# Decode layer on one core: paired copies of transposed K, constants on GpSimd, aligned programs, and w_gate's first row in two pieces

## The chip, the cores and the metric

The kernel runs on one core of one Trainium2 chip. The metric is device time in microseconds of one execution. A comparison of kernels uses the median of several executions on the same chip.

## The reference

One token for each of two batch entries goes through an attention layer and a feed-forward layer. All inputs are bf16; D = 640, 32 heads of 192, a cache of 8192 positions of which the last 2048 are used, F = 1536.

```python
def _A_ref(x, k_cache, v_cache, wq, wo):      # B=2, Sq=1, D=640, Hq=Hkv=32, Sk=8192, Dh=192
    W = min(4096, max(256, Sk // 4))          # 2048
    q = (x @ wq).reshape(B, Sq, 32, 192).transpose(0, 2, 1, 3)
    k = k_cache[:, :, Sk - W:, :]
    v = v_cache[:, :, Sk - W:, :]
    p = _softmax(einsum("bhqd,bhkd->bhqk", q, k) * (192 ** -0.5))
    o = einsum("bhqk,bhkd->bhqd", p, v)
    return o.transpose(0, 2, 1, 3).reshape(B, Sq, 32 * 192) @ wo

def _B_ref(x, w_gate, w_up, w_down):
    return (_gelu(x @ w_gate) * (x @ w_up)) @ w_down

h = x + _A_ref(_layernorm(x), k_cache, v_cache, wq, wo)
out = h + _B_ref(_layernorm(h), w_gate, w_up, w_down)
```

Nearly all of the work is reading: 16 loads of K and 16 of V of 3 MB each, wq (7.5 MB), wo (four loads of 1.9 MB), and the three feed-forward matrices of 1.9 MB each.

## The kernel before

**Groups.** The 2 x 32 heads are worked in 16 groups (NG) of four heads of one batch entry. J counts blocks of four groups. For group g, one load brings K of the four heads into a ring in SBUF (128 partitions, 24576 bytes each), another brings V.

**Per group.** `transposes(g, half)` turns K on TensorE, two bf16 at a time as one f32, 48 transposes of 128x128 per group: twelve steps n, each of four transposes into one of four PSUM banks `tps[0..3]` in turn, and then one copy of 128x1024 bf16 into `ktr`, by ScalarE (ACT) for n in (2, 3, 5, 8, 11) and by VectorE (DVE) for the other seven. `scores(g)` multiplies `ktr` by the masked query `rq` (made four groups ahead by `q_masked` on GpSimd). DVE takes the maximum, `softmax(g)` takes the exponent on ACT, `e_columns(g)` turns it, and `pv(g)` multiplies by V. The order on TensorE is: first half of the transposes of g, `e_columns(g-1)`, second half, `pv(g-1)`, `scores(g)`, `softmax(g)`. After every fourth group `z_rows`, `o_rows`, `o_columns` and `oproj` normalise the block and add its part of `@ wo`.

**Who orders what.** `_Prog` records the operations of each engine in program order and works out which semaphore waits are needed; `emit` writes the program of one engine, and `emit_loop` writes that of TensorE as a loop over J with four passes. `load` puts a transfer on a list, and `pump` issues it on SyncE's queue (SP) as soon as the ring bytes that it overwrites have been used, in the order of the list: K0, wq, K1, V0, K2, V1 and so on, then wo, w_gate, w_up and w_down. ACT issues two transfers of its own at the very start: `load_wg0` (L379), row 0 of each partition's five rows of w_gate into its own tile `wgh`, 128 partitions of 3072 bytes, and x into `xrow`.

**Constants.** Masks, selectors and identity matrices are made on the chip. GpSimd makes index ramps (`ci`, `pi`, `ei`), bit masks (`bits`) and zeros; DVE makes everything else from them between the first layer norm and the first K copies, and a second set in `consts_late`, recorded after `q_stationary` and ahead of `scores(0)`.

**The end.** After group 15: `e_columns(15)`, `z_rows(3)`, `pv(15)`, `o_rows(3)`, `oproj(2)`, `o_columns(3)`, `oproj(3)`, the second layer norm, the gate product (`ffn_in`, which reads `wgh` first), the up product, and w_down in four pieces, each as soon as it has landed. DVE copies the result (L862) and SP sends it out (L863).

Of the kernel before, what the change touches and what calls it, by code (L numbers as in the profile page):

```python
# [216 lines left out]
TPG = 64  # L217
WDC = ((0, 6), (6, 9), (9, 11), (11, 12))
# [9 lines left out]
def bass_sequential_preLN__sliding_block_cached__geglu_ffn__decode_kernel(  # L228
# [12 lines left out]
    with ExitStack() as ctx:  # L241
# [79 lines left out]
        tps = [ps(f"tps{i}", [128, 512], F32) for i in range(4)]  # L321
# [123 lines left out]
        dve(lambda e: e.memset(eps_t[:, :], EPS), W=["eps"])  # L445
        dve(lambda e: e.memset(onesd[:, :], 1.0 / D), W=["onesd"])
        act(lambda e: e.preload_act_table_set("natural_log_exp_and_others"))


        dve(lambda e: e.memset(xnT[:, :, :].rearrange("p a b -> p (a b)").bitcast(I32), 0), W=["xnT"])  # L450
# [21 lines left out]
        def _x_T(e):  # L472
# [10 lines left out]
        dve(tt(pti[:, :], pi[:, :].to_broadcast([128, 11]), bits[:, :], ALU.bitwise_and),  # L483
            R=["pi"] + [("bits", k) for k in range(11)], W=["pti"])
        dve(lambda e: e.tensor_copy(pf[:, :], pti[:, :]), R=["pti"], W=["pf"])
# [10 lines left out]
        dve(ts(pg[:, 1:2], rb(31), 16.0, ALU.is_lt), R=["pf"], W=["v16"])  # L496
        dve(ts(pg[:, 2:3], rb(31), 4.0, ALU.is_lt), R=["pf"], W=["v4"])
        dve(ts(pg[:, 4:5], rb(16), 8.0, ALU.mult, rb(3), ALU.add), R=["pf"], W=["c16"])
        dve(ts(pg[:, 5:6], rb(96), 0.125, ALU.mult, pg[:, 4:5], ALU.add), R=["pf", "c16"], W=["c16b"])
        dve(ts(pg[:, 6:7], rb(96), 0.5, ALU.mult, rb(1), ALU.add), R=["pf"], W=["c64"])  # L500
        dve(ts(pg[:, 7:8], rb(12), 0.5, ALU.mult, pg[:, 6:7], ALU.add), R=["pf", "c64"], W=["c64b"])
        dve(ts(pg[:, 6:7], rb(2), 4.0, ALU.mult, pg[:, 7:8], ALU.add), R=["pf", "c64b"], W=["c64"])
        dve(ts(pg[:, 7:8], rb(16), 64.0, ALU.mult, pg[:, 6:7], ALU.add), R=["pf", "c64"], W=["c64b"])
        dve(ts(pg[:, 8:9], rb(96), 1.0 / 32.0, ALU.mult), R=["pf"], W=["cq"])
        dve(ts(pg[:, 9:10], rb(6), rb(1), ALU.add), R=["pf"], W=["cqa"])
        dve(ts(pg[:, 9:10], pg[:, 9:10], 4.0, ALU.mult, pg[:, 8:9], ALU.add), R=["cqa", "cq"], W=["cqb"])
        dve(ts(pg[:, 10:11], rb(64), 1.0 / 16.0, ALU.mult, rb(31), ALU.add), R=["pf"], W=["chd"])
        dve(ts(pg[:, 11:12], rb(3), 2.0, ALU.mult), R=["pf"], W=["p3"])
        dve(ts(pg[:, 12:13], rb(32), rb(31), ALU.add, 16.0, ALU.mult), R=["pf"], W=["c63"])

        dve(ts(selq[:, :], cf[:, 0, 0:32], pg[:, 9:10], ALU.is_equal), R=["cf0", "cqb"], W=["selq"])
        dve(lambda e: e.tensor_copy(ef[:, :], ei[:, :]), R=["ei"], W=["ef"])
        for r in range(5):
            dve(ts(ge[:, :, r], ef[:, :], 192.0 * r, ALU.is_ge), R=["ef"], W=[("ge", r)])
        dve(tt(mask[:, :, :], ge[:, :, 0:4], ge[:, :, 1:5], ALU.subtract), R=[("ge", r) for r in range(5)], W=["mask"])

        dve(ts(pm[:, :], cf[:, 3, :], rb(28), ALU.is_equal), R=["cfm", "pf"], W=["pm"])
        dve(ts(oh16[:, :], cf[:, 0, 0:16], pg[:, 5:6], ALU.is_equal), R=["cf0", "c16b"], W=["oh16"])
        dve(ts(sel64[:, :], cf[:, 0, 0:64], pg[:, 7:8], ALU.is_equal), R=["cf0", "c64b"], W=["sel64"])
        dve(ts(mask16[:, :], cf[:, 2, 0:16], pg[:, 11:12], ALU.is_equal), R=["cfm", "p3"], W=["mask16"])  # L520
        dve(ts(mska[:, :], cf[:, 1, :], 4.0, ALU.mult, rb(12), ALU.is_equal), R=["cfm", "pf"], W=["mska"])
        dve(ts(zsel[:, :], mska[:, :], pg[:, 1:2], ALU.mult), R=["mska", "v16"], W=["zsel"])
        dve(ts(mska[:, :], mska[:, :], -1.0, ALU.add, BIG, ALU.mult), R=["mska", "zsel"], W=["mska"])

        dve(lambda e: e.memset(lsx[:, :, :], 0.0), W=["lsx"])
        dve(lambda e: e.memset(sps[:, :], 0.0), X=["s"])
        dve(lambda e: e.memset(m1[:, :], 0.0), X=["m1"])

        def consts_late():
            dve(ts(oh4[:, :], cf[:, 0, 0:4], pg[:, 8:9], ALU.is_equal), R=["cf0", "cq"], W=["oh4"])  # L530
            dve(ts(cf[:, 1, :], cf[:, 1, :], 2.0, ALU.mult), R=["cfm", "mska"], W=["cf1"])
            dve(ts(cf[:, 4, :], cf[:, 4, :], 0.25, ALU.mult), R=["cfm"], W=["cf4"])
            dve(tt(cf[:, 1, :], cf[:, 1, :], cf[:, 4, :], ALU.add), R=["cf1", "cf4"], W=["cf1"])
            dve(ts(cf[:, 3, :], cf[:, 3, :], 1000.0, ALU.mult), R=["cfm", "pm"], W=["cf3"])
            dve(tt(cf[:, 1, :], cf[:, 1, :], cf[:, 3, :], ALU.add), R=["cf1", "cf3"], W=["cf1"])
            for tp in range(2):
                dve(ts(selw[:, tp, :], cf[:, 1, :], float(tp), ALU.add, rb(31), ALU.is_equal), R=["cf1", "pf"], W=[("selw", tp)])
            dve(ts(bsel[:, :], cf[:, 0, 0:2], rb(31), ALU.is_equal, 1.0 / D, ALU.mult), R=["cf0", "pf"], W=["bsel"])
            for h in range(2):
                dve(ts(hsel[:, h, :], cf[:, 0, 0:17], 512.0 * h, ALU.add, pg[:, 12:13], ALU.is_equal), R=["cf0", "c63"], W=[("hsel", h)])  # L540
            dve(ts(pg[:, 8:9], rb(32), 1.0 / 32.0, ALU.mult), R=["pf", "cqb", "oh4"], W=["cb"])
            dve(ts(selb[:, :], cf[:, 0, 0:2], pg[:, 8:9], ALU.is_equal, pg[:, 2:3], ALU.mult), R=["cf0", "cb", "v4"], W=["selb"])
            dve(ts(maskhd[:, :], cf[:, 0, 0:8], pg[:, 10:11], ALU.is_equal, pg[:, 2:3], ALU.mult),
                R=["cf0", "chd", "v4"], W=["maskhd"])
# [4 lines left out]
        def transposes(g, half):  # L549

            kk, ktoks = where["k", g]
            kv = kk.bitcast(F32)
            for n in range(6 * half, 6 * half + 6):
                c, ch = n % 3, n // 3
                bi = tb_count[0] % 4
                tb_count[0] += 1

                def fn(e, c=c, ch=ch, bi=bi):
                    for u in range(4):
                        off = 128 * (3 * (4 * ch + u) + c)  # L560
                        ins = e.transpose(tps[bi][:, 128 * u:128 * (u + 1)], kv[:, off:off + 128], identf[:, :])  # L561
                    return ins

                pe(fn, R=ktoks + ["identf"], X=[("t", bi)])
                if n == 11:
                    done(("k", g))
                bv = tps[bi][:, :].bitcast(BF16)
                dst = ktr[:, c, 1024 * ch:1024 * (ch + 1)]
                if n in (2, 3, 5, 8, 11):
                    act(lambda e, dst=dst, bv=bv: e.activation(out=dst, in_=bv, func=ACT.Copy),  # L570
                        W=[("kt", n)], X=[("t", bi)])
                else:
                    dve(lambda e, dst=dst, bv=bv: e.tensor_copy(dst, bv), W=[("kt", n)], X=[("t", bi)], cls=0)  # L573
# [41 lines left out]
        def scores(g):  # L615
# [8 lines left out]
            pe(fn, R=[("rq", g % 4)] + [("kt", n) for n in range(12)], X=["s"])  # L624
# [242 lines left out]
        P.resolve({("dve", 0): 4 * 11, ("dve", 1): 8, ("act", 0): 4 * 6, ("pool", 0): 4})  # L867
# [40 lines left out]
```

## Time and profile before

| | |
|---|---|
| median of 3 runs (lowest to highest) | 292.94 us (292.78 to 292.95) |
| the profiled execution | 293.0 us, of which its span is 291.4 |
| mean granted TensorE clock | 0.858 |
| moved by DMA | 122.44 MB, 420 GB/s over the span |
| busy: PE, DVE, ACT, POOL | 194.3, 128.6, 96.0, 8.6 us |
| K transposes on PE (L561) | 768 in 114.9 us; idle before them 45.7, of it 42.9 for K's loads |
| K copies on DVE (L573) and ACT (L570) | 112 of 688 ns, 80 of 1023 ns |

The profile is of one execution. "Busy" is the sum of an engine's instructions. A line of the page's groups gives line, engine, operation, the tiles out<-in, how many, the busy time, the mean of one, and then the idle time of the engine just before them with what ended most of it. In the DMA section, q1 is SP's queue, q10 ACT's, and "instruction" marks transfers that bring program code. The chain is followed back from the last instruction, at each step to what released it.

### The profile page before, as it was taken

What the parts mean: (1) busy time and instruction counts of PE and PEld (TensorE: products, weight loads), DVE (VectorE), ACT (ScalarE), POOL (GpSimd) and SP (SyncE); (2) the same over time, 40 slices, a digit from 0 to 9 for tenths busy, and PEclk for the clock granted to TensorE, in tenths of its full rate; (3) what the DMA queues carried; (4) which work ended last, traced back from release to release, by engine and by line L of the source; (5) the groups of instructions that cost most, each with busy time, mean ns of one, the idle gap of its engine ahead of it and who ended that gap; (6) DMA issues with size and microseconds to landing.
All of it is one profiled execution on the core that took longest, in us unless ns stands there. A gap on an engine that the chain in (4) does not pass through costs nothing.

```text
span 291.4 us, 5056 instructions
## 1 busy us (share of the span) xinstructions
PE 194.3 (67%) x2141; PEld 150.9 (52%) x2141; DVE 128.6 (44%) x311; ACT 96.0 (33%) x120; POOL 8.6 (3%) x36
## 2 busy tenths in 40 slices
PE   1570759747768197849496496749496977494585
PEld 1560436727466195628284475447475855472342
DVE  4761075623537144616156154434365534352332
ACT  1142016623442143616143063416161634251001
POOL 4000020000000000000000000000000000000000
PEclk9998699995979579998869599968897799897955
DMA  8999999999999999999999999999999999999994
GB/s 324 432 440 422 427 432 431 428 427 432 427 418 441 432 432 430 428 432 432 432 413 449 428 428 428 432 432 428 428 432 425 432 432 432 432 428 419 421 414 174
DMA packets 6506, 122.44 MB, mean 420 GB/s; under 512 B 734, under 2 KB 864, under 8 KB 1504
## 3 DMA queue, kind: packets, MB, share of 16 engines
q1 hardware_dynamic: 6348, 121.90, 97.8%
q10 hardware_dynamic: 148, 0.40, 0.5%
q8 instruction: 7, 0.11, 0.2%
q14 instruction: 3, 0.02, 0.0%
HBM read 122.29 MB, written 0.00 MB: 420 GB/s over the span
## 4 chain that ended last, share of the span: by engine, by line
DMA 76%; PE 19%; SPq 2%; DVE 1%; issue 0%
DMA ring<-in_A_k_cache_dram 57%; PE tps L561 15%; DMA ring<-in_A_wq_dram 10%; DMA ring<-in_B_w_down_dram 9%; PE tps L582 2%; SPq L348 2%; PE ops L663 1%; PE m L714 1%; PE m L696 1%; DVE ktr L573 0%; DVE ering L413 0%; PE m L856 0%; PE m L647 0%; PE m L677 0%; DVE yrow L862 0%
## 5 line engine op out<-in xcount | busy, mean ns | idle before, releaser
L561 PE MATMUL tps<-identf,ring 128*128 128x128 f32 x768 | 114.9, 318 | 45.7 <-DMA ring<-in_A_k_cache_dram 42.9
L561 PEld LDWEIGHTS tps<-identf,ring 128*128 128x128 f32 x768 | 106.1, 167 | 49.3 <-DMA ring<-in_A_k_cache_dram 44.2
L570 ACT ACTIVATE ktr<-tps 128x1024 bf16<-128x1024 bf16 x80 | 79.2, 1023 | 85.0 <-PE tps L561 85.0
L573 DVE COPY ktr<-tps 128x1024 bf16<-128x1024 bf16 x112 | 74.4, 688 | 72.9 <-PE tps L561 72.2
L638 ACT ACTIVATE eexp<-sm,nm 128x512 bf16<-128x512 f32 x16 | 11.5, 721 | 65.2 <-DVE nm L636 65.2
L663 PE MATMUL ops<-ring,ering 128*32 128x384 bf16 x512 | 25.0, 340 | 6.0 <-DMA ring<-in_A_v_cache_dram 6.0
L627 DVE CUSTOM_DVE_ANT_1 sm<-sps,mska 128x512 f32<-128x512 f32 x16 | 11.1, 691 | 35.9 <-PE sps L619 35.9
L619 PE MATMUL sps<-ktr,rq 128*16 128x512 bf16 x384 | 24.6, 388 | 1.1 <-POOL rq L413 1.1
L663 PEld LDWEIGHTS ops<-ring,ering 128*32 128x32 bf16 x512 | 12.7, 99 | 14.8 <-DMA ring<-in_A_v_cache_dram 7.6
L619 PEld LDWEIGHTS sps<-ktr,rq 128*16 128x16 bf16 x384 | 9.2, 88 | 11.4 <-POOL rq L413 1.2
L634 PEld LDWEIGHTS m<-mrhs,pm 128*128 128x128 bf16 x16 | 1.5, 95 | 23.4 <-DVE mrhs L409 23.4
L634 PE MATMUL m<-mrhs,pm 128*128 128x16 bf16 x16 | 2.9, 183 | 15.7 <-DVE mrhs L409 15.7
L413 POOL TENSOR_TENSOR rq<-qs,mask 128x96 bf16<-128x96 bf16 x16 | 5.6, 359 | 195.5 <-PE sps L619 161.3
L582 PE MATMUL tps<-ring,xnT 128*32 128x384 bf16 x80 | 5.5, 455 | 7.7 <-DMA ring<-in_A_wq_dram 7.7
L582 PEld LDWEIGHTS tps<-ring,xnT 128*32 128x32 bf16 x80 | 3.1, 131 | 9.9 <-issue 7.9
L413 DVE TENSOR_TENSOR ering<-m,mask 128x256 bf16<-128x256 f32 x16 | 6.7, 419 | 2.2 <-PE m L647 2.0
L605 DVE CAST qs<-ops 128x384 bf16<-128x384 f32 x1 | 0.6, 558 | 14.1 <-PE ops L600 14.1
L714 PE MATMUL m<-ring,ot 128*2 128x320 bf16 x96 | 4.1, 307 | 2.5 <-DMA ring<-in_A_wo_dram 2.5
L794 ACT ACTIVATE lnv<-tps,eps_t 98x1 f32<-98x1 f32 x1 | 0.3, 261 | 16.6 <-PE tps L792 16.6
L647 PE MATMUL m<-sel,eexp 128*128 128x64 bf16 x64 | 4.7, 200 | 1.2 <-ACT eexp L638 1.2
L413 DVE TENSOR_TENSOR orow<-m,wm 128x1536 bf16<-128x1536 f32 x3 | 5.3, 1751 | 0.0
L673 DVE COPY osb<-ops 128x192 f32<-128x192 f32 x8 | 2.5, 353 | 6.0 <-PE ops L663 6.0
(126 smaller groups left out, 85.6 us busy)
## 6 DMA issues: line engine op xcount, KB each, us to landing
ring<-in_A_k_cache_dram SPq DMA_DIRECT2D x16, 3072.0 KB, 31.7
ring<-in_A_v_cache_dram SPq DMA_DIRECT2D x16, 3072.0 KB, 27.4
ring<-in_A_wq_dram SPq DMA_DIRECT2D x1, 7680.0 KB, 28.6
ring<-in_A_wo_dram SPq DMA_DIRECT2D x4, 1920.0 KB, 21.9
ring<-in_B_w_gate_dram SPq DMA_DIRECT2D x1, 1536.0 KB, 31.5
ring<-in_B_w_up_dram SPq DMA_DIRECT2D x1, 1536.0 KB, 23.8
ring<-in_B_w_down_dram SPq DMA_DIRECT2D x1, 960.0 KB, 26.3
ring<-in_B_w_down_dram SPq DMA_DIRECT2D x1, 480.0 KB, 27.0
```

Source lines behind the costliest of these rows:

```text
L348: P.op("sp", lambda e, v=v, src=src: e.dma_start(v, src), W=toks + [("sem", sem)], dma=sem)
L413: return lambda e: e.tensor_tensor(out=out, in0=a, in1=b, op=op)
L561: ins = e.transpose(tps[bi][:, 128 * u:128 * (u + 1)], kv[:, off:off + 128], identf[:, :])
L570: act(lambda e, dst=dst, bv=bv: e.activation(out=dst, in_=bv, func=ACT.Copy), W=[("kt", n)], X=[("t", bi)])
L573: dve(lambda e, dst=dst, bv=bv: e.tensor_copy(dst, bv), W=[("kt", n)], X=[("t", bi)], cls=0)
L582: ins = e.matmul(tps[0][32 * r:32 * (r + 1), 0:384], lhsT=xnT[:, c, 32 * J:32 * (J + 1)], rhs=wq[:, c, 1536 * J + 384 * r:1536 * J + 384 * ...
L619: ins = e.matmul(sps[32 * ch:32 * ch + 16, :], lhsT=rq[:, g % 4, k, :], rhs=ktr[:, k // 2, 1024 * ch + k % 2:1024 * (ch + 1):2], start=(k ...
L627: dve(lambda e: e.tensor_tensor_reduce(out=sm[:, :].rearrange("p (u x) -> p u x", u=4), in0=sps[:, :].rearrange("p (u x) -> p u x", u=4), ...
L638: act(lambda e: e.activation(out=eexp[:, :], in_=sm[:, :], func=ACT.Exp, bias=nm[:, 0:1], scale=1.0, accum_out=zr[:, g % 4:g % 4 + 1]), R= ...
L647: ins = e.matmul(o, lhsT=eexp[:, 128 * u:128 * (u + 1)], rhs=sel64[:, :], start=True, stop=True)
L663: ins = e.matmul(ops_[32 * r:32 * (r + 1), 0:384], lhsT=ering[:, g % 4, t, :], rhs=vv[:, 384 * t:384 * (t + 1)], start=(g % 4 == 0 and t < 4),
L714: ins = e.matmul(m1[32 * r:32 * r + 2, 192:512], lhsT=ot[:, kk, :], rhs=wo[:, kk - k0, 320 * h:320 * (h + 1)], start=(kk == 1 or J < 2 and ...
```

## The change

Four things change.

- The four PSUM banks become two tiles `tpp[0..1]` of two banks each. `transposes` now has three steps per half, each of eight transposes into one of the two tiles, and one copy of 128x2048: DVE for the first and third step (channels 0 and 1 of one quarter), ACT for the middle one (channel 2 of two quarters).
- The constants that DVE made, all but the first few, are made by GpSimd; four of them directly as index ramps instead of by masking bits. Some memsets and the bit tests on DVE move ahead of the identity matrix.
- `addr_align` places what follows it in the programs of GpSimd, DVE and ACT at a fixed place against a block of 128 instructions: GpSimd and ACT at its start, DVE at place 120. For ACT it stands behind its DMA issues. At most two fillers are executed; a longer gap is jumped over.
- `load_wg0` issues two transfers, partitions 100 to 127 and then 0 to 99, with a semaphore each, instead of one of 128.

```diff
+WGP = 100
...
-        tps = [ps(f"tps{i}", [128, 512], F32) for i in range(4)]
+        tpp = [ps(f"tpp{i}", [128, 1024], F32) for i in range(2)]
+        tps = [tpp[i // 2][:, 512 * (i % 2):512 * (i % 2 + 1)] for i in range(4)]
...
         def load_wg0():
-            where["wg", 0] = wgh[:, :, :], ["wgh"]
-            P.op("act", lambda e: e.dma_start(wgh[:, 0, :], B_w_gate.rearrange("(p c) f -> p c f", c=NC5)[:, 0, :]), W=["wgh"], dma="wg0")
+            where["wg", 0] = wgh[:, :, :], [("wgh", 0), ("wgh", 1)]
+            src = B_w_gate.rearrange("(p c) f -> p c f", c=NC5)
+            for i, (p0, p1) in enumerate(((WGP, 128), (0, WGP))):
+                P.op("act", lambda e, p0=p0, p1=p1: e.dma_start(wgh[p0:p1, 0, :], src[p0:p1, 0, :]), W=[("wgh", i)], dma=f"wg0{i}")
...
+        dve(lambda e: e.memset(eps_t[:, :], EPS), W=["eps"])
+        dve(lambda e: e.memset(onesd[:, :], 1.0 / D), W=["onesd"])
+        dve(lambda e: e.memset(xnT[:, :, :].rearrange("p a b -> p (a b)").bitcast(I32), 0), W=["xnT"])
+        dve(lambda e: e.memset(lsx[:, :, :], 0.0), W=["lsx"])
+        dve(lambda e: e.memset(sps[:, :], 0.0), X=["s"])
+        dve(lambda e: e.memset(m1[:, :], 0.0), X=["m1"])
         dve(lambda e: e.tensor_copy(cf[:, 0, :], ci[:, :]), R=["ci"], W=["cf0"])
         dve(lambda e: e.tensor_copy(pg[:, 0:1], pi[:, :]), R=["pi"], W=["row"])
+        dve(tt(pti[:, :], pi[:, :].to_broadcast([128, 11]), bits[:, :], ALU.bitwise_and),
+            R=["pi"] + [("bits", k) for k in range(11)], W=["pti"])
+        dve(lambda e: e.tensor_copy(pf[:, :], pti[:, :]), R=["pti"], W=["pf"])
...
-        for k, m in enumerate((3, 6, 28, 96)):
-            dve(ts(cti[:, k, :], ci[:, :], m, ALU.bitwise_and), R=["ci"], W=[("cti", k)])
-        dve(lambda e: e.tensor_copy(cf[:, 1:5, :], cti[:, :, :]), R=[("cti", k) for k in range(4)], W=["cfm"])
+        for k, pat in enumerate(([[0, 32], [1, 4]], [[0, 16], [2, 4], [0, 2]], [[0, 4], [4, 8], [0, 4]], [[32, 4], [0, 32]])):
+            pool(lambda e, k=k, pat=pat: e.iota(cti[:, k, :], pattern=pat, base=0, channel_multiplier=0), W=[("cti", k)])
+        pool(lambda e: e.tensor_copy(cf[:, 1:5, :], cti[:, :, :]), R=[("cti", k) for k in range(4)], W=["cfm"])
...
-        dve(ts(selq[:, :], cf[:, 0, 0:32], pg[:, 9:10], ALU.is_equal), R=["cf0", "cqb"], W=["selq"])
+        pool(ts(selq[:, :], cf[:, 0, 0:32], pg[:, 9:10], ALU.is_equal), R=["cf0", "cqb"], W=["selq"])
...
         def consts_late():
-            dve(ts(oh4[:, :], cf[:, 0, 0:4], pg[:, 8:9], ALU.is_equal), R=["cf0", "cq"], W=["oh4"])
+            pool(ts(oh4[:, :], cf[:, 0, 0:4], pg[:, 8:9], ALU.is_equal), R=["cf0", "cq"], W=["oh4"])
...
-            for n in range(6 * half, 6 * half + 6):
-                c, ch = n % 3, n // 3
-                bi = tb_count[0] % 4
+            for k in range(3):
+                bi = tb_count[0] % 2
                 tb_count[0] += 1
+                banks = [(2, 2 * half), (2, 2 * half + 1)] if k == 1 else [(0, 2 * half + k // 2), (1, 2 * half + k // 2)]
...
-                if n in (2, 3, 5, 8, 11):
-                    act(lambda e, dst=dst, bv=bv: e.activation(out=dst, in_=bv, func=ACT.Copy),
-                        W=[("kt", n)], X=[("t", bi)])
+                bv = tpp[bi][:, :].bitcast(BF16)
+                if k == 1:
+                    dst = ktr[:, 2, 2048 * half:2048 * (half + 1)]
+                    act(lambda e, dst=dst, bv=bv: e.activation(out=dst, in_=bv, func=ACT.Copy), W=[("kt", half, k)], X=both)
                 else:
-                    dve(lambda e, dst=dst, bv=bv: e.tensor_copy(dst, bv), W=[("kt", n)], X=[("t", bi)], cls=0)
+                    ch = 2 * half + k // 2
+                    dst = ktr[:, 0:2, 1024 * ch:1024 * (ch + 1)]
+                    dve(lambda e, dst=dst, bv=bv: e.tensor_copy(dst, bv.rearrange("p (a x) -> p a x", a=2)), W=[("kt", half, k)],
+                        X=both, cls=0)
...
+        nc.gpsimd.addr_align(128, 0, 2)
         P.emit("pool", nc.gpsimd, sems)
+        nc.vector.addr_align(128, 120, 2)
         P.emit("dve", nc.vector, sems)
-        P.emit("act", nc.scalar, sems)
+        P.emit("act", nc.scalar, sems, P.per["act"][:3])
+        nc.scalar.addr_align(128, 0, 2)
+        P.emit("act", nc.scalar, sems, P.per["act"][3:])
```

The lines left out move the other constants from `dve(...)` to `pool(...)` unchanged.

More of the change, by code (lines that the diff above doesn't have):

```diff
@@ L512, in bass_sequential_preLN__sliding_block_cached__geglu_ffn__decode_kernel @@
-        dve(lambda e: e.tensor_copy(ef[:, :], ei[:, :]), R=["ei"], W=["ef"])
-        for r in range(5):
[L514 to L518, printed above, removed]
@@ new lines, in bass_sequential_preLN__sliding_block_cached__geglu_ffn__decode_kernel @@
+        pool(ts(pg[:, 7:8], rb(12), 0.5, ALU.mult, pg[:, 6:7], ALU.add), R=["pf", "c64"], W=["c64b"])
+        pool(ts(pg[:, 6:7], rb(2), 4.0, ALU.mult, pg[:, 7:8], ALU.add), R=["pf", "c64b"], W=["c64"])
+        pool(ts(pg[:, 7:8], rb(16), 64.0, ALU.mult, pg[:, 6:7], ALU.add), R=["pf", "c64"], W=["c64b"])
+        pool(ts(pg[:, 8:9], rb(96), 1.0 / 32.0, ALU.mult), R=["pf"], W=["cq"])
+        pool(ts(pg[:, 9:10], rb(6), rb(1), ALU.add), R=["pf"], W=["cqa"])
+        pool(ts(pg[:, 9:10], pg[:, 9:10], 4.0, ALU.mult, pg[:, 8:9], ALU.add), R=["cqa", "cq"], W=["cqb"])
@@ new lines, in bass_sequential_preLN__sliding_block_cached__geglu_ffn__decode_kernel @@
+        pool(tt(mask[:, :, :], ge[:, :, 0:4], ge[:, :, 1:5], ALU.subtract), R=[("ge", r) for r in range(5)], W=["mask"])
+        pool(ts(pm[:, :], cf[:, 3, :], rb(28), ALU.is_equal), R=["cfm", "pf"], W=["pm"])
+        pool(ts(oh16[:, :], cf[:, 0, 0:16], pg[:, 5:6], ALU.is_equal), R=["cf0", "c16b"], W=["oh16"])
+        pool(ts(sel64[:, :], cf[:, 0, 0:64], pg[:, 7:8], ALU.is_equal), R=["cf0", "c64b"], W=["sel64"])
+        pool(ts(mask16[:, :], cf[:, 2, 0:16], pg[:, 11:12], ALU.is_equal), R=["cfm", "p3"], W=["mask16"])
@@ L544, in consts_late @@
+            pool(ts(pg[:, 8:9], rb(32), 1.0 / 32.0, ALU.mult), R=["pf", "cqb", "oh4"], W=["cb"])
+            pool(ts(selb[:, :], cf[:, 0, 0:2], pg[:, 8:9], ALU.is_equal, pg[:, 2:3], ALU.mult), R=["cf0", "cb", "v4"], W=["selb"])
+            pool(ts(maskhd[:, :], cf[:, 0, 0:8], pg[:, 10:11], ALU.is_equal, pg[:, 2:3], ALU.mult),
                 R=["cf0", "chd", "v4"], W=["maskhd"])
@@ L552, in transposes, with fn @@
             kv = kk.bitcast(F32)
-            for n in range(6 * half, 6 * half + 6):
-                c, ch = n % 3, n // 3
-                bi = tb_count[0] % 4
+            for k in range(3):
+                bi = tb_count[0] % 2
                 tb_count[0] += 1
[L558 to L561, printed above, removed]
-                    return ins
-                pe(fn, R=ktoks + ["identf"], X=[("t", bi)])
-                if n == 11:
+                banks = [(2, 2 * half), (2, 2 * half + 1)] if k == 1 else [(0, 2 * half + k // 2), (1, 2 * half + k // 2)]
+                def fn(e, banks=banks, bi=bi):
+                    for j, (c, ch) in enumerate(banks):
+                        for u in range(4):
+                            off = 128 * (3 * (4 * ch + u) + c)
+                            ins = e.transpose(tpp[bi][:, 512 * j + 128 * u:512 * j + 128 * (u + 1)], kv[:, off:off + 128], identf[:, :])
+                    return ins
+                both = [("t", 2 * bi), ("t", 2 * bi + 1)]
+                pe(fn, R=ktoks + ["identf"], X=both)
+                if half == 1 and k == 2:
                     done(("k", g))
-                bv = tps[bi][:, :].bitcast(BF16)
-                dst = ktr[:, c, 1024 * ch:1024 * (ch + 1)]
-                if n in (2, 3, 5, 8, 11):
-                    act(lambda e, dst=dst, bv=bv: e.activation(out=dst, in_=bv, func=ACT.Copy),
-                        W=[("kt", n)], X=[("t", bi)])
-                else:
-                    dve(lambda e, dst=dst, bv=bv: e.tensor_copy(dst, bv), W=[("kt", n)], X=[("t", bi)], cls=0)
+                bv = tpp[bi][:, :].bitcast(BF16)
+                if k == 1:
+                    dst = ktr[:, 2, 2048 * half:2048 * (half + 1)]
+                    act(lambda e, dst=dst, bv=bv: e.activation(out=dst, in_=bv, func=ACT.Copy), W=[("kt", half, k)], X=both)
+                else:
+                    ch = 2 * half + k // 2
+                    dst = ktr[:, 0:2, 1024 * ch:1024 * (ch + 1)]
+                    dve(lambda e, dst=dst, bv=bv: e.tensor_copy(dst, bv.rearrange("p (a x) -> p a x", a=2)), W=[("kt", half, k)],
+                        X=both, cls=0)
         def q_rows():
@@ L622, in fn @@
                 return ins
-            pe(fn, R=[("rq", g % 4)] + [("kt", n) for n in range(12)], X=["s"])
+            pe(fn, R=[("rq", g % 4)] + [("kt", n, k) for n in range(2) for k in range(3)], X=["s"])
             if g + 4 < NG:
```

62 lines of the change are left out of this document (22 added, 40 removed).

## The prediction

> **What bounds the kernel now.** I read the page's queues and chain first, then the waits, then the timeline of the last microseconds, then the trace's records of when each load's semaphore rises. The queues and the chain:
>
> ```profile
> DMA packets 6506, 122.44 MB, mean 420 GB/s; under 512 B 734, under 2 KB 864, under 8 KB 1504
> q1 hardware_dynamic: 6348, 121.90, 97.8%
> q10 hardware_dynamic: 148, 0.40, 0.5%
> q8 instruction: 7, 0.11, 0.2%
> q14 instruction: 3, 0.02, 0.0%
> DMA 76%; PE 19%; SPq 2%; DVE 1%; issue 0%
> ```
>
> The 16 DMA engines are busy 98.5% of the span: one stream of loads sets the time, and 76% of the chain is that stream. Besides data they carry ten instruction fetches. What PE waits for:
>
> ```profile
> PE tps L561 <- DMA ring<-in_A_k_cache_dram: 42.9, 15, 7.0
> PE m L634 <- DVE mrhs L409: 15.7, 16, 2.1
> PE tps L561 <- DVE ktr L573: 2.1, 1, 2.1
> ```
>
> PE waits for K before 15 of 16 groups, 42.9/15 = 2.9 us each; it is not the bound. The end:
>
> ```profile
> 288.55 0.71 PE L856 MATMUL m<-ring,uT 128*17 128x160 bf16 x12
> 288.94 0.10 PEld L856 LDWEIGHTS m<-ring,uT 128*17 128x17 bf16 x4 [0.28 <-DMA ring<-in_B_w_down_dram]
> 289.31 0.33 DVE L862 CAST yrow<-m 113x160 bf16<-113x160 f32 x1 [2.26 <-PE m L856]
> 289.66 0.69 SPq L863 DMA_DIRECT2D out_dram<-yrow  x1
> ```
>
> PE waits for the last w_down piece, landed at 288.90; 2.5 us later the span ends. So the question is when the slowest of the 16 engines ends its share.
>
> The trace records each engine's increment of a load's semaphore, sixteen per 128-row load. For the first K load they lie between 10.82 and 11.23 us, for the last w_down load between 286.91 and 288.90: eight at 286.91 to 287.25, one at 287.88, six at 288.48 to 288.65, one at 288.90. Their mean is 287.80: perfect balance would be worth 1.1 us. The spread grows in steps, each after a fetch. Followed packet by packet, the 16 KB fetches at 34.3, 50.6, 61.5, 78.0, 91.2 and 274.8 us each put a different engine 1.5 us back (0.29 to 1.82 against the earliest, 0.18 to 1.70, and so on). The 8 KB fetches at 17.4 and 150.1 put one and the same engine back 0.9 and 1.0: it is the last, 2.1 late. The one at 110.1 costs a third kind of engine 0.7. So: six engines 1.65 to 1.9 late, one 2.1, one 1.0, eight up to 0.4.
>
> **The change, part by part.** *Aligned programs.* The 8 KB fetches come with 57 and 177 DVE instructions started (120 apart), the middle one with 48 ACT instructions: I read the first pair as DVE's, the other as ACT's, about 128 instructions per 8 KB. As built, DVE's program shrinks from 316 to 224 instructions, ACT's from 109 to 63, GpSimd's grows from 41 to 92, and each is moved to a fixed place against a block of 128: GpSimd and ACT at its start, DVE eight instructions before it. Each then crosses its first boundary in the first 2 us, where most engines have no packet yet (the first starts at 1.74). ACT and GpSimd do not come to a second one; DVE does, after 136 instructions, near group 10. So ACT's fetch at 110.1 and DVE's at 17.4 leave the stream, DVE's second stays: its engine falls from 2.1 to 1.2 late. An early fetch that meets data costs between 0 and 0.9; I take 0, as engines idle there. Without more, the last engine would be a 16 KB one at 1.88: 0.24 us gained. PE's program loses 15 instructions of some 930; its fetches stay.
>
> *w_gate's first row.* x's two rows leave two increments with data and one at once (1.99 us), the output's outer four leave four and one at once, 128 rows leave sixteen. From that I infer that a load runs on the largest number of engines up to 16 that divides its rows: 28 on 14 engines, two rows each; 100 on ten, ten rows each. If both start at the same first engine, ten engines carry 12 rows, four carry 2, two none, instead of 8 each. A 3072 B packet takes 121 ns, so +0.48, -0.73 and -0.97 us, from the first microseconds to the end. The other bound is an even spread, with no shift. I take the first, nearest to the rows with 2 and 4.
>
> [...]
>
> *Which engines are late* decides the sign. If the six late ones are the six that are relieved, they end at 1.88 - 0.73 = 1.15 or less; untouched ones at 0.45 + 0.48 = 0.93; DVE's at 1.2 + 0.48 = 1.68 if it is among the ten. No 16 KB fetch hits an engine twice, so they go round the engines in some order; and x's two engines, which are among the first ten, seem free of them (two neighbours lie only 3 ns apart, so this is not sure). Both speak for a run of late engines away from the first ones; neither says that it ends at the last six. I take this case, as the weakest step of the sum, with DVE's engine among the ten: 2.12 - 1.68 = 0.44 us gained. Everything behind moves along: the last part starts from the wo load at 275.89, and o_columns ends at 273.77, 2.1 us before it.
>
> *Paired K copies.* Per group seven DVE copies of 688 ns (4.8 us) become four of twice the size; five ACT copies of 1023 ns (5.1 us) become two. Their price lies between once and twice the old one; with a fixed part of 0.15 us taken off I estimate 1.22 and 1.88 us. DVE then has 4.9 us per group, ACT 3.8. But PE has two buffers of eight transposes instead of four of four. At 111 ns per transpose (24 in 2.67 us) a fill takes 0.89; working D-A-D on two buffers through, a group's last copy ends 8.1 us after K lands instead of 6.9; at half clock (24 in 5.2) 11.9 instead of 11.4. So +0.4 to +1.2 us, under the 2.9 us wait for K. For the loads the cover is larger still: the shortest lead of an issue on SP before the previous load's first increment is 7.3 us (K2, at 35.7). At the last group the cover is PE's 0.82 us wait for V15 at 266.70 and then the 2.1 us before wo: 2.9 us. Past that it costs one for one.
>
> *Constants on GpSimd.* Some 50 small instructions leave DVE (9.4 to 16.4 us) and start on GpSimd after 3.6. Its rows range from 98 ns (memset 128x1) to 359 ns (128x96): 5 to 18 us, so done by 22 at the latest against the first use at 36, where wq's product ends. consts_late stands behind the first four q_masked on GpSimd's queue and ahead of the fifth, needed only four groups later. Cost 0; if the cover were gone, scores(0) would be late and PE's K waits would absorb it.
>
> *One more DMA issue on ACT*: 0.38 us ahead of x and of ACT's table load. x's chain ends at 9.5 and is needed at 30.1, when wq lands. Cost 0. The early DVE memsets and pf stand ahead of identf by under 2 us: the same cover.
>
> Sum: the profiled execution took 293.0, 1.6 beside its span; the median is 292.94. 292.94 - 0.44 = 292.5.
>
> **Rivals.** *All late engines relieved* (R1): DVE's engine is among the six, or its second fetch falls away; the last is then 1.15 late: 2.12 - 1.15 = 0.97 gained, 291.97. For: DVE's second boundary lies only 88 instructions before its program's end, so nothing may be left to fetch. Against: ACT's fetch at 110.1 came with little left of its program too, and with DVE's engine seven are late and only six relieved.
>
> *The split does nothing* (R2): rows spread evenly, only the fetches count: 292.7. [...]
>
> *The late engines are loaded further* (R3, slower): a 16 KB engine is among the first ten: 1.88 + 0.48 = 2.36 late, +0.24; if it also carries an early fetch or PE's last one (286.4 us, now behind its engine's data), another 0.7 to 1.5 less what is idle, up to +1. It decides as soon as one 16 KB engine lies among the ten. Likeliest 293.2. For: two of the late engines got their first w_gate rows among the early ones.
>
> *The pair of buffers becomes the bound* (R4, slower): copies at twice the price (1.38 and 2.05 us) and a lag carried over several groups pass the 2.9 us before wo: +0.5 to +2, say 293.9. For: the group after a block's end waits only 0.4 us for K (at 115.77). Against: the others make it up, at 2.9 on average.
>
> **How the numbers follow.** Forecast 38%, R1 25%, R2 7%, R3 20%, R4 10%. What a measurement of this kernel can tell from no change is about 0.2%, 0.59 us: faster is below 292.35, slower above 293.53. R1 gives 24 points of faster and the forecast's edge 8; R3 gives 8 points of slower and R4 10; the rest is within. The range 291.9 to 293.5 takes in R1, the forecast, R2 and R3 without its tail. The forecast's own range is 292.2 to 292.8.
>
> **What would show it.** The instruction queues of the page fall from ten in-span packets to about eight or nine, with none of 8 KB between 3 and 150 us. The sixteen increments of the last w_down load spread over 1.7 us or less instead of 2.0, and the last lands near 288.5. The wgh rows run on 14 and 10 engines: ten data increments for the second piece. DVE copies of 1.2 us x64, ACT of 1.9 x32; PE's K waits fall to about 30 us and stay above zero before each group. Wrong if the last landing is at 289 or later (R3), if PE stops waiting for K or SP issues a load with less than 2 us of lead (R4), or if DMA idles before 288.

## The result, and the profile after

The changed kernel takes 294.72 us (median of 6 runs, 294.71 to 295.03) against 292.99 us for the kernel before on the same chip (6 runs, 292.78 to 293.11): ratio 1.006, 95% interval 1.005 to 1.0071. It is slower by 1.73 us, outside the predicted range. Its profiled execution took 294.71 us with a span of 293.3; before it was 293.0 with 291.4.

The page's DMA section and the chain's shares, by engine and then by line:

```profile
DMA packets 6515, 122.45 MB, mean 417 GB/s; under 512 B 742, under 2 KB 872, under 8 KB 1512
q1 hardware_dynamic: 6348, 121.90, 97.8%
q10 hardware_dynamic: 156, 0.40, 0.4%
q14 instruction: 4, 0.03, 0.0%
DMA 61%; PE 23%; DVE 10%; ACT 2%; SPq 1%; issue 1%; POOL 1%; ACTq 0%
DMA ring<-in_A_k_cache_dram 43%; PE tpp L562 17%; DMA ring<-in_B_w_down_dram 9%; DMA xrow<-in_A_x_dram 9%; DVE ktr L576 7%; ACT ktr L572 2%; PE ops L667 2%; SPq L350 1%; PE tpp L586 1%; PE sps L623 1%; DVE ering L417 1%; DVE sm L631 1%; PE m L718 1%; PE m L700 1%; POOL rq L417 0%
```

The same 121.90 MB fill the engines for the same share of a longer span: the mean rate fell from 420 to 417 GB/s. The stream did not get holes worth speaking of; it got slower somewhere. What PE waits for (line, releaser, total us, times, longest):

```profile
PE m L482 <- DMA xrow<-in_A_x_dram: 27.4, 1, 27.4
PE tpp L562 <- DMA ring<-in_A_k_cache_dram: 21.1, 10, 5.1
PE tpp L562 <- DVE ktr L576: 9.2, 21, 0.4
```

The first line is new: x lands at 27.25 us instead of 5.67, and PE stands still until then. PE starts 21 us late and catches up until about group 5. The waits for K are halved, but most of that is not x: in the kernel with one piece below, which keeps the rest of the change and has x early, they are 29.2 us, so of the 21.8 us that are gone 13.7 go with the rest of the change and 8.1 with the late start. From the timeline between 24 and 46 us:

```profile
27.38 0.33 PE L482 MATMUL m<-identb,xrow 2*128 2x2 bf16 x5 [27.38 <-DMA xrow<-in_A_x_dram]
39.62 3.43 PE L586 MATMUL tpp<-ring,xnT 128*32 128x384 bf16 x80 [0.44 <-ACT ktr L572]
43.11 0.54 SPq L350 DMA_DIRECT2D ring<-in_A_k_cache_dram  x1
```

SP's issue of K2 in the kernel before:

```profile
35.71 0.54 SPq L348 DMA_DIRECT2D ring<-in_A_k_cache_dram  x1
```

The product with wq ends at 43.1 instead of 35.7, and K2's issue comes that much later. It was the one with the shortest lead: SP is now done with it at 43.65, 1.2 us before V0's first increment at 44.85, where it had 7.3 us. The end of the span looks as before:

```profile
290.86 0.10 PEld L860 LDWEIGHTS m<-ring,uT 128*17 128x17 bf16 x4 [0.29 <-DMA ring<-in_B_w_down_dram]
291.19 0.33 DVE L866 CAST yrow<-m 113x160 bf16<-113x160 f32 x1 [1.88 <-PE m L860]
291.54 0.69 SPq L867 DMA_DIRECT2D out_dram<-yrow  x1
```

The last w_down increment lands at 290.82 instead of 288.90 (+1.92) and the tail behind it is unchanged, so the loss is all in the stream. An increment, as in the prediction, is one engine's report that its share of a load has landed. The mean of each load's sixteen increments, against the kernel before, is late by 1.02 us at K0, 1.77 at wq, 1.67 at K1, 1.77 at V0, 2.00 at K2, 2.12 at V1 and 2.06 at the end. So 1.7 to 1.8 us are lost by 30 us, about 0.3 at K2, and nothing after that.

How the first part is lost shows in the packets between 4 and 10 us. The DMA view of that window gives for each queue the packets, the MB and their time as a share of 16 engines' window. Before:

```profile
q1 hardware_dynamic: 112, 2.75, 106.7%
q10 hardware_dynamic: 4, 0.00, 0.2%
```

After:

```profile
q1 hardware_dynamic: 86, 2.11, 91.2%
q10 hardware_dynamic: 47, 0.14, 6.4%
```

Share times 96 us (16 engines, 6 us), divided by packets, is the mean time of one K0 packet of 24576 B: 0.915 us before, 1.018 after. The engines are as busy (16.1 at a time before, 16.0 after), but each packet takes longer, and so do wq's packets (2.3 to 2.65 us instead of 2.27) until the last w_gate row has gone at about 20 us. Between 6 and 8 us every one of the 28 recorded K0 packets took 992 ns or more, where before all took 912, though six of the sixteen engines carry no row of the second piece (its semaphore shows ten increments with data and one at once).

### The profile page after: what moved, and what is told of

Its sections match the earlier page's. It is cut to its first block, busy times and chain, and to the rows that moved or that the text cites. A ratio compares the mean times of both kernels' runs of the same rounds, so it can differ in the third digit from the quotient of the medians.

```text
span 293.3 us, 4910 instructions
## 1 busy us (share of the span) xinstructions
PE 194.3 (66%) x2141; PEld 145.4 (50%) x2141; DVE 123.3 (42%) x215; ACT 76.9 (26%) x72; POOL 25.4 (9%) x84
## 3 DMA queue, kind: packets, MB, share of 16 engines
q1 hardware_dynamic: 6348, 121.90, 97.8%
## 4 chain that ended last, share of the span: by engine, by line
DMA 61%; PE 23%; DVE 10%; ACT 2%; SPq 1%; issue 1%; POOL 1%; ACTq 0%
DMA ring<-in_A_k_cache_dram 43%; PE tpp L562 17%; DMA ring<-in_B_w_down_dram 9%; DMA xrow<-in_A_x_dram 9%; DVE ktr L576 7%; ACT ktr L572 2%; PE ops L667 2%; SPq L350 1%; PE tpp L586 1%; PE sps L623 1%; DVE ering L417 1%; DVE sm L631 1%; PE m L718 1%; PE m L700 1%; POOL rq L417 0%
## 5 line engine op out<-in xcount | busy, mean ns | idle before, releaser
L562 PE MATMUL tpp<-identf,ring 128*128 128x128 f32 x768 | 114.9, 312 | 35.1 <-DMA ring<-in_A_k_cache_dram 21.1
L562 PEld LDWEIGHTS tpp<-identf,ring 128*128 128x128 f32 x768 | 102.2, 163 | 43.0 <-DMA ring<-in_A_k_cache_dram 22.0
L576 DVE COPY ktr<-tpp 128x2048 bf16<-128x2048 bf16 x64 | 78.4, 1224 | 85.5 <-PE tpp L562 85.5
L572 ACT ACTIVATE ktr<-tpp 128x2048 bf16<-128x2048 bf16 x32 | 60.1, 1877 | 90.3 <-PE tpp L562 90.3
L667 PE MATMUL ops<-ring,ering 128*32 128x384 bf16 x512 | 23.9, 329 | 0.0
L473 ACT ACTIVATE lt<-m,eps_t 128x2 f32<-128x2 f32 x1 | 0.3, 262 | 26.6 <-PE m L471 26.6
L718 PE MATMUL m<-ring,ot 128*2 128x320 bf16 x96 | 5.6, 384 | 1.8 <-DMA ring<-in_A_wo_dram 1.8
L700 PE MATMUL m<-selb,orow 128*128 128x2 bf16 x48 | 3.5, 199 | 4.5 <-DVE ering L417 4.5
L700 PEld LDWEIGHTS m<-selb,orow 128*128 128x128 bf16 x48 | 3.2, 160 | 5.4 <-DVE ering L417 4.9
```

What stands on the lines that cost most here:

```text
L562: ins = e.transpose(tpp[bi][:, 512 * j + 128 * u:512 * j + 128 * (u + 1)], kv[:, off:off + 128], identf[:, :])
L576: dve(lambda e, dst=dst, bv=bv: e.tensor_copy(dst, bv.rearrange("p (a x) -> p a x", a=2)), W=[("kt", half, k)], X=both, cls=0)
L667: ins = e.matmul(ops_[32 * r:32 * (r + 1), 0:384], lhsT=ering[:, g % 4, t, :], rhs=vv[:, 384 * t:384 * (t + 1)], start=(g % 4 == 0 and t < 4),
L700: ins = e.matmul(m2[:, 2 * kk:2 * kk + 2], lhsT=orow[:, :, kk:DH:12], rhs=selb[:, :], start=True, stop=True)
L718: ins = e.matmul(m1[32 * r:32 * r + 2, 192:512], lhsT=ot[:, kk, :], rhs=wo[:, kk - k0, 320 * h:320 * (h + 1)], start=(kk == 1 or J < 2 and ...
```

## The experiments

Theory at the start: the second piece of w_gate's row (100 rows on ten engines) meets K0's packets; it slows them, and x, queued behind it, is late. Rivals: GpSimd's constants disturb the stream in its first 17 us; the early program fetches do (after the change 8 KB fetches fall at 4.6 and 6.7 us); the two-buffer copies make K2's issue late. In this table "packet" is the mean time of a K0 packet that starts between 4 and 10 us, worked out as above, and "wq" how late the mean of wq's increments is against the kernel before; "x lands" is x's last increment. The edits are shown shortened.

| kernel | us | ratio to before (95%) | packet, us | wq, us | x lands, us |
|---|---|---|---|---|---|
| changed | 294.72 | 1.006 (1.005 to 1.0071) | 1.018 | +1.77 | 27.3 |
| one piece | 292.83 | 0.9988 (0.9979 to 0.9997) | 0.921 | +0.14 | 6.4 |
| one piece, programs unaligned | 292.99 | 0.9996 (0.9987 to 1.0005) | 0.912 | +0.03 | 5.6 |
| before, split only | 298.55 | 1.0169 (1.0144 to 1.0195) | 0.985 | +1.35 | 26.4 |
| before, split and constants | 294.73 | 1.0053 (1.004 to 1.0067) | 0.999 | +1.64 | 26.6 |
| changed, x first | 295.26 | 1.0074 (1.006 to 1.0088) | 1.028 | +2.16 | 2.2 |
| large piece first | 294.40 | 1.0041 (1.0027 to 1.0055) | 1.055 | +1.56 | 11.0 |
| halves of 64 | 294.12 | 1.0035 (1.0021 to 1.0049) | 1.015 | +1.13 | 13.1 |
| even and odd partitions | 293.17 | 0.9999 (0.999 to 1.0008) | 0.926 | +0.48 | 12.3 |
| halves of the source, alternating destination | 293.15 | 1.0003 (0.9993 to 1.0012) | 0.922 | +0.39 | 12.1 |
| alternating source, halves of the destination | 294.19 | 1.0037 (1.0026 to 1.0049) | 1.069 | +1.61 | 13.3 |
| alternating, other engines | 294.14 | 1.0035 (1.0021 to 1.0049) | 0.995 | +1.05 | 17.2 |
| one piece, issued late | 293.34 | 1.0008 (0.9999 to 1.0017) | 0.936 | +0.59 | 2.1 |

**Which part of the change costs.** One piece again, the rest of the change kept:

```
-            for i, (p0, p1) in enumerate(((WGP, 128), (0, WGP))):
-                P.op("act", lambda e, p0=p0, p1=p1: e.dma_start(wgh[p0:p1, 0, :], src[p0:p1, 0, :]), ...)
+            P.op("act", lambda e: e.dma_start(wgh[:, 0, :], B_w_gate.rearrange(...)[:, 0, :]), W=["wgh"], dma="wg0")
```

> The changed kernel with w_gate's first row as one transfer of 128 partitions again; the paired copies, the constants on GpSimd and the aligned programs stay. Theory (the second piece of the row meets K0's packets, and x lands at 27 us behind it): x lands at 5.5 to 6.5 us, PE starts by 7, K2's issue is again over 4 us ahead of the stream, and the time is 292.5 to 293.2 us. Rivals: if GpSimd's constants slow the stream in its first 17 us, or the early 8 KB fetches do, the loads stay late by over 1 us at K1 and the time is 294.0 to 294.7. If the two-buffer copies make K2's issue late, the time is 293.5 to 294.5 with K2's issue still after 40 us.

292.83 us. With constants on GpSimd, early fetches and paired copies all in place the packets are at 0.921 us, so none of these slows the stream: the split is the loss. Its waits:

```profile
PE tpp L560 <- DMA ring<-in_A_k_cache_dram: 29.2, 11, 5.3
PE m L480 <- DMA xrow<-in_A_x_dram: 6.5, 1, 6.5
```

PE has x at 6.5 us and waits for K as long in total as predicted. The same kernel without the three alignments, to see what they are worth:

> The changed kernel with the row as one piece and without the aligned programs; paired copies and constants on GpSimd stay. The one-piece kernel took 292.83. If the aligned programs take two 8 KB fetches out of the stream for 0.24 us, as the prediction has it: 293.0 to 293.2, with 8 KB fetches after 15 us. If their early fetches cost as much as they save: 292.7 to 292.95.

292.99 us, with 8 KB fetches at 15.1, 92.6, 176.7 and 240.6 us. The time lies between the two ranges of the expectation, and the intervals of the two kernels overlap: the runs don't decide it.

The counterpart, the kernel before with nothing but the two pieces:

> The kernel before with nothing but the split of w_gate's first row (partitions 100 to 127, then 0 to 99). Theory: x lands at 25 to 28 us, PE starts behind it, and the time is 294.2 to 295.0, all of the change's loss. Rivals: if constants, fetches or copies cause the loss, the time is 292.8 to 293.2 here.

298.55 us: it loses 5.4, far more than expected. Its packets are slow like the changed kernel's. The rest is a hole that the page shows in the seventh slice of 7.4 us, and K2's issue on SP's timeline:

```profile
GB/s 287 447 402 416 423 401 164 426 428 455 426 418 413 431 436 450 426 426 423 423 439 427 449 426 423 423 423 439 439 439 426 423 423 423 443 439 417 415 417 178
47.64 0.54 SPq L349 DMA_DIRECT2D ring<-in_A_k_cache_dram  x1
```

K2 is issued at 47.64, when everything issued earlier has all but landed (V0's last increment 46.50); K2's increments come 4.8 us later than V0's delay explains. Adding only the constants' move to GpSimd to this kernel tells why:

> The kernel before with the split and the constants on GpSimd, but with its four-buffer copies and unaligned programs. The split alone took 298.55. Theory: there the constants on VectorE stood behind the layer norm that waits for x, so the K0 copies and K2's issue came 5 us late; with the constants off VectorE that goes and the time is 294.4 to 295.3, about the changed kernel's. Rival: the paired copies rescued it, and the time stays at 297.5 to 299.

```profile
40.92 0.54 SPq L349 DMA_DIRECT2D ring<-in_A_k_cache_dram  x1
```

294.73 us, the changed kernel's time. On VectorE the constants stand behind the layer norm that waits for x, and ahead of K0's copies; off it, K2 leaves 6.7 us earlier and the hole is gone. The rival (the paired copies rescue it) falls: they are not in this kernel. Here x is as late as in the changed kernel, yet K2 leaves 2.2 us before the changed kernel's 43.11 and its increments are no later than V0's (+1.54 after +1.65). So the changed kernel's 0.3 us at K2 appear where x is late and the copies have two buffers; with the paired copies and an early x (next run) they don't appear.

**Is it x's delay?** x's transfer ahead of both pieces:

```
-        load_wg0()
         P.op("act", lambda e: e.dma_start(xrow[0:2, :], A_x[:, 0, :]), W=["xrow"], dma="dx")
+        load_wg0()
```

> The changed kernel with x's transfer issued ahead of the two pieces, so that x waits behind nothing. Theory in two parts: x lands by 5 us, PE starts by 7 and K2 is issued in time, which takes away the gap at K2 (0.3 to 0.8 us); the 100 rows still alternate with K0's packets and still make wq's last landing 1.5 to 2 us late, so the time is 293.8 to 294.4. If the late x is the whole cause, 292.6 to 293.2. If x's lateness costs nothing, 294.6 to 294.8.

```profile
PE tpp L586 <- DMA ring<-in_A_wq_dram: 10.3, 1, 10.3
PE m L482 <- DVE identb L457: 5.1, 1, 5.1
```

295.26 us, and its interval overlaps the changed kernel's. PE starts at 5.1, waits for wq again, K2 is issued at 38.6, and the step at K2 is gone: the mean delay is 2.16 at wq and 2.04 at K2. But the rows now run until 25 us, wq is even later, and the time is no better. It lies above all three ranges of the expectation, which had the step at K2 right and took the rows' cost for 1.5 to 2 us. A chain that gives 9% to x's transfer named a wait that was not the cause of the lost time.

**Uneven engines, order, or something else?**

```
-            for i, (p0, p1) in enumerate(((WGP, 128), (0, WGP))):
+            for i, (p0, p1) in enumerate(((0, WGP), (WGP, 128))):       # large piece first
+            for i, (p0, p1) in enumerate(((64, 128), (0, 64))):         # halves
+            for i, (p0, p1) in enumerate(((0, 128), (1, 128))):         # even and odd, with p0:p1:2
```

Each of the three kernels has one of the + lines. The third cuts the row into two pieces of 64 partitions, the even and the odd ones. By their increments the loads of 128, 100 and 28 rows go over 16, 10 and 14 engines, each time the largest number up to 16 that divides the rows; by that count 64 rows lie on 16 engines, 4 on each, in this cut and in the halves. Theory B of its expectation takes it that in this cut each engine writes only partitions that are its own in K0 too, which no run records.

> The changed kernel with its two pieces in the other order: 100 rows (10 engines, 10 rows each) first, then 28 rows (14 engines, 2 rows each). The bytes per engine are the same as in the change. If the cost lies in the rows that alternate with K0's and wq's packets: only 2 rows per engine meet K0, x lands at 5.5 to 8 us, K0's packets are slow for 2 to 3 us, and the time is 292.8 to 293.4. If the uneven bytes per engine are the cost: x lands early, and the time stays at 294.2 to 295.2.

> The changed kernel with the row cut in two halves of 64 partitions, both of which go over all 16 engines with 4 rows each. If the uneven spreading (10 engines with 10 rows each) is the cause: the second piece meets only the first 4 or so packets of each engine, x lands at 7 to 11 us, the time is 292.7 to 293.4. If any second piece behind K0 costs what this one does, whatever its engines: 294.3 to 294.8. If constants, fetches or copies cause the loss: 294.3 to 294.8 with x landing early.

> [...] Theory A (two queues that alternate slow all packets, whatever they write): K0's packets take 1000 to 1120 ns while the rows run, x lands at 11 to 14 us, and the time is that of the halves, 293.9 to 294.4 us. Theory B (an engine that writes partitions which another engine is writing in K0 makes both wait): K0's packets stay at 912 to 940 ns, x lands at 8 to 12 us, and the time is 292.7 to 293.4.

Large first:

```profile
q1 hardware_dynamic: 86, 2.11, 94.5%
q10 hardware_dynamic: 47, 0.09, 4.8%
```

294.40 us, in the range that the expectation gives to uneven bytes. It is not the clean case that the expectation had in mind: the first piece is not done when K0's packets begin at 2.9 us, and 52 of its rows still run beside them until 4.2 us. The 28 rows of the second piece run from 5.3 to 8.1 us, and all 28 recorded K0 packets that start between 6 and 8 us take 1036 ns or more. Halves: 294.12, between the ranges of the expectation. By the count above every engine carries the same bytes here, and the stream is still 1.13 us late at wq, so unevenness is not the main cause. Even and odd: 293.17. This cut has the same number of pieces, of rows per engine and of rows that meet K0 as the halves. The DMA view of 4 to 10 us, halves and then even and odd:

```profile
q1 hardware_dynamic: 92, 2.26, 97.3%
q10 hardware_dynamic: 62, 0.19, 8.1%
```

```profile
q1 hardware_dynamic: 94, 2.31, 90.7%
q10 hardware_dynamic: 64, 0.20, 8.1%
```

As many packets of both queues; 1.015 us each in the one, 0.926 in the other. In the even and odd cut two queues alternate and cost little: 0.926 us a packet against 0.915 in the kernel before. Either the source's addresses or the destination's partitions differ in a way that matters, and two kernels cross them. In both, w_gate's rows stand in other partitions than the program expects, so the output is not the reference's; they serve for the times alone:

```
+   e.dma_start(wgh[i:128:2, 0, :], src[p0:p1, 0, :])    # alternating destination
+   e.dma_start(wgh[p0:p1, 0, :], src[i:128:2, 0, :])    # alternating source
```

> The cut into two pieces of 64 rows, with rows 64 to 127 of the source written to the even partitions and rows 0 to 63 to the odd ones (so w_gate's rows stand in other partitions than the reference's). The halves took 294.12 us with K0's packets at 1040 to 1140 ns while the second piece ran, the alternating pieces 293.17 with packets at 912. [...] If the source's addresses decide: packets at 1040 to 1140 and 293.9 to 294.5.

> The counterpart: the even rows of the source written to partitions 64 to 127, the odd ones to 0 to 63 (again not the reference's order of rows). If the destination's partitions decide: K0's packets at 1040 to 1140 ns and 293.9 to 294.5 us, as with the halves. If the source's addresses decide: packets at 912 to 930 and 292.9 to 293.5.

```profile
q1 hardware_dynamic: 95, 2.33, 91.2%
q10 hardware_dynamic: 67, 0.20, 8.2%
```

```profile
q1 hardware_dynamic: 86, 2.11, 95.8%
q10 hardware_dynamic: 59, 0.18, 8.1%
```

Alternating destination: 0.922 us per packet and 293.15. Alternating source: 1.069 and 294.19. The destination decides.

**Spread, or whose partition?** The rows could be harmless because they are spread over all partitions, or because each is written by the engine that writes its partition in K0 too. Two last kernels:

```
+            for i, (p0, p1) in enumerate(((1, 128), (8, 128), (0, 8))):   # p0:p1:2: 64, 60 and 4 rows
```

> Three pieces over alternating partitions: the 64 odd ones, then the 60 even ones from 8 to 126 (15 engines, 4 rows each, so other engines than in the cut of 64 and 64), then the 4 even ones from 0 to 6. It tells apart two readings of the runs so far. If it is enough that the rows are spread over all 128 partitions: K0's packets at 912 to 930 ns and 293.0 to 293.5 us. If each row must be written by the engine that also writes its partition in K0: packets at 1000 to 1150 ns and 293.8 to 294.5 us, as with the halves.

```
+        P.op("act", ... xrow ...)
+        act(lambda e: e.preload_act_table_set("natural_log_exp_and_others"))
+        load_wg0()                                                         # one piece of 128 partitions
```

> The changed kernel with the row as one piece of 128 partitions, but issued late on ScalarE's queue: x first, then the load of ScalarE's table, then the row, so that all of its 128 rows (8 per engine, of the same shape as K0, so each engine writes the partitions that it writes in K0) alternate with K0's packets. If two queues that alternate slow the packets whatever they write: K0's packets at 1000 ns and more and 294 to 295 us. If it is only rows that another engine's partitions get: packets at 912 to 930 and 292.7 to 293.3 us.

```profile
q1 hardware_dynamic: 94, 2.31, 97.4%
q10 hardware_dynamic: 59, 0.18, 7.8%
```

```profile
q1 hardware_dynamic: 85, 2.09, 82.9%
q10 hardware_dynamic: 86, 0.26, 11.0%
```

With 60 rows instead of 64 in the second piece, spread just as widely but dealt to 15 engines instead of 16 (fifteen increments with data and one at once), the packets are slow again (0.995 us; 989 ns or more in all that start between 8 and 10 us) and the time is 294.14. With all 128 rows among K0's packets, but in K0's own shape, they stay at 912 ns for the most part (0.936 us in the mean), at 293.34; mean and time lie just above the expected 912 to 930 ns and 292.7 to 293.3. The reading that fits all runs is that the rows slow the stream when an engine writes to partitions that belong to another engine in K0. That the split costs the time, and that the destination's partitions decide, is shown; the owner is inferred. Which engine wrote which partition is not recorded; that it is the same one in K0 and in a piece of 128 partitions is the author's assumption, from the same shape, and for the even and odd cut it is inferred from the packet times. Why a row to another engine's partitions slows the packets, no run here shows.

## Why the prediction was wrong, point by point

*What bounds the kernel* was right: the stream sets the time, and the loss is in it, microsecond for microsecond.

*w_gate's first row* is the step that failed. Its rows did go over 14 and 10 engines, as inferred: the first piece leaves 14 increments with data and one at once, the second 10 and one. But the step moved 3072 B packets at 121 ns from engine to engine (+0.48, -0.73, -0.97) as if their sum stayed zero and nothing else changed. Measured, it is +1.77 us on the mean of all engines by 30 us. The recorded bytes say how it is made up: 0.3 us between 2 and 6 us, where fewer engines are busy around the gap between the pieces (10 and 13 in the two halves of 2 to 3 us, instead of 16), and 1.4 from 6 to 22, where the engines are full but move 377 to 422 GB/s instead of 431 to 434. The even and odd cut loses 0.48, of which 0.37 lie before 6 us: almost only the first kind. The step put the second kind at nothing, and it is the larger one.

*Which engines are late* was the basis of the forecast's gain of 0.44 us and could not decide it. It took the last engine as 2.12 us late, which the loads up to wo show; at the last load it is 1.99. The last load's increments do spread less, 1.72 us instead of 1.99, so the last engine is 1.92 later where the mean is 2.06 later: a gain of 0.14. With the same two pieces the spread is 2.13 with the large one first, 2.87 with x first and 2.81 in the kernel with split and constants. The relief is small and not dependable. That the ten engines are the first ones, with x's two among them and the late ones elsewhere, was the author's assumption; which engine a packet ran on is not recorded.

*One more DMA issue on ACT* counted the issue (x's is at 1.70 instead of 1.15) and wrote cost 0, with x's chain done at 9.5. What was missed is that x stands behind the second piece in the same queue, whose rows alternate with K0's and wq's packets: one row per packet of 1.0 and then 2.3 to 2.6 us makes ten rows take until 20 us, and x lands at 27.25. That cut the lead of K2 from 7.3 to 1.2 us and cost 0.3 us there; in the kernel before with the split it costs 3.8 more as long as the constants stay on VectorE (298.55 against 294.73).

*Constants on GpSimd*, cost 0: right while x is early, and done at 16.6 us, inside the 22 given. With the split it is worth those 3.8 us, which the step did not see, since x's delay was not seen.

*Paired K copies*: the estimates of 1.22 and 1.88 us were right.

```profile
L576 DVE COPY ktr<-tpp 128x2048 bf16<-128x2048 bf16 x64 | 78.4, 1224 | 85.5 <-PE tpp L562 85.5
L572 ACT ACTIVATE ktr<-tpp 128x2048 bf16<-128x2048 bf16 x32 | 60.1, 1877 | 90.3 <-PE tpp L562 90.3
```

The fixed part, estimated at 0.15 us, came out at 152 ns on DVE (2 x 688 - 1224) and 169 on ACT (2 x 1023 - 1877). With one piece their cover holds: PE still waits 29.2 us for K in all, near the 30 predicted, and the one-piece kernels are not slower than the kernel before. But it does not wait before each group, as was stated: eleven waits are left of fifteen, and none before groups 2, 6 and 10, so there K is no longer what PE waits for. R4 did not happen as a loss, except for the 0.3 us at K2 when x is late. One of its marks, an issue with less than 2 us of lead, was met in the changed kernel (K2, 1.2 us), through the late x: with one piece K2 leaves at 36.25 instead of 43.11.

*Aligned programs*: the fetches at 17.4 and 110.1 are gone, and one of 8 KB stays, at 172.2, as predicted. The early ones fell at 1.76, 4.60 and 6.69, two of them among data, against "none between 3 and 150". With the seven of 16 KB the span holds eleven fetches, against eight or nine predicted and ten before. What the alignment gains is not settled: 292.83 with and 292.99 without it, intervals that overlap; the 0.24 us of the step are neither shown nor excluded.

Of the rivals, R3 had the sign and not the mechanism: it loads late engines with 0.48 us more, where the whole stream lost speed. R2's time (292.7) came near what the change does without its split (292.83). The mark set for "wrong", a last landing at 289 or later, was met at 290.82.

The one-piece kernel beats both, but over the kernel before by only 0.12% (0.03 to 0.21), 0.28 us, at the edge of what can be told; the two profiles don't show where, since the last load lands no earlier in it (288.99).

## What to carry to other kernels

In this kernel a stream of 128-partition loads fills all engines, and what the row beside it cost went by the partitions that it wrote: the ratio to the kernel before is 1.006 with pieces of 28 and 100, 0.9999 with even and odd partitions, and 1.0008 with all 128 rows in K0's shape among its packets. In a kernel like it, try a transfer beside the stream in the stream's own shape, or so early that it is nearly over when the stream starts (in the kernel before the rows start between 1.74 and 3.40 us, K0's first packet at 3.08). A small transfer queued behind one that runs beside the stream waits with it: x, behind ten rows per engine that went one per stream packet of 1.0 and then 2.3 to 2.6 us, landed at 27.25 us instead of 5.67. When you place one, count that wait and ask what starts with it. And before believing a long wait at the head of the chain, take it away: here that was 27 us of waiting, and without it the time was no better (295.26 us against 294.72).

## What the runs showed of the hardware

- K0's packets of 24576 B take 912 ns in the kernel before. Beside rows of 3072 B to neighbouring partitions they took 992 to 1268 ns in the changed kernel (all 28 that start between 6 and 8 us) and 1135 to 1201 with alternating source (all 23 between 8 and 10 us). Beside the even and odd cut and beside rows in K0's own shape most stayed at 912 (85 of 94 and 65 of 85 between 4 and 10 us).
- In the changed kernel engines without rows are slowed too: between 7.5 and 8 us fourteen engines at a time carry K0 packets, all of them of 992 ns or more, and ten have rows. If each of the sixteen engines owns eight of K0's 128 partitions, which is the author's assumption, 100 rows lie in the shares of at least 13, so an engine without rows can still own partitions that others write. Why all packets are slowed is not settled.
- The slowing does not go by the number of rows: by the recorded bytes the 28 rows of the large-first kernel's second piece cost 0.62 us of the stream after 6 us, the 64 rows of the halves 0.64.
- Two queues on one engine took turns packet by packet, whatever the sizes: in the changed kernel the second piece's rows start in groups of about ten, 1.0 us apart among K0's packets of 24 KB and 2.4 to 2.6 us apart among wq's of 60 KB. Which engine a packet ran on is not recorded; the turns are read from the spacing.
